# Converting 64-bit weights: ScalarE takes both halves of a chunk at once, and GpSimd takes the integer addition for w_in

## The chip, the cores and the metric

The kernel runs on one core of a Trainium2 chip. The metric is the device time of one execution in microseconds; before the change the median of 3 runs is 906.83 us (906.54 to 906.88). The core's engines run side by side, each with its own queue of instructions in a fixed order: TensorE (PE; its weight loads are PEld), VectorE (DVE), ScalarE (ACT), GpSimd (POOL) and SyncE (SP), which issues most transfers. An instruction at the head of a queue that waits for another engine holds back all that stands behind it. Matmuls write into PSUM; the other tiles live in SBUF, and a tile's slot can be given to a new tile when the last reader of the old one is done.

## The reference

Attention with softmaxes on q (over the head dimension) and on k (over the sequence), then a feed-forward layer with a squared ReLU:

```python
q_s = softmax(q, axis=-1); k_s = softmax(k, axis=2)      # 8 batches, 8 heads, 576 rows, 64 columns
kv  = einsum('bhsd,bhse->bhde', k_s, v)
x   = einsum('bhsd,bhde->bhse', q_s, kv)                 # as 4608 tokens of 512
h   = maximum(x @ w_in, 0.0)                             # w_in  512 x 2048
out = (h * h) @ w_out                                    # w_out 2048 x 512
```

q, k and v are float32. The weights arrive as float64, since their scale factor is a float64, and the kernel reads them as 64-bit words.

## The kernel before

The tokens go in 9 tiles of 512: tile t holds the first 512 rows of batch t, and tile 8 the last 64 rows of all batches. For each tile the FFN runs over 16 chunks `f` of 128 columns of the hidden layer. `first` makes `h` of a chunk (12 matmuls of 128x512: each product is three, with high and low parts of both factors, in the order high x high, high x low, low x high), ScalarE makes `r` (ReLU) from it and VectorE squares it in PSUM; `split_g` makes `gh` on ScalarE and the rest `gl` on VectorE; `second` adds 12 matmuls to four accumulators `acc`, which hold the tile's output. While tile t goes through its FFN, the attention of batch t + 1 is made between the chunks, one pair of heads `p` for each four chunks: `k_max`, `kmT`, `dg` and `kmb` (the maximum of k over the rows, turned and spread by TensorE), `ek` and `kt` (exponentials), `kv`, `qT`, `x`.

The weights are converted once. A chunk has a w_in half and a w_out half, each 128 partitions x 512 words of 64 bits. `load_words` loads them, `scale_words` lets ScalarE scale the high 32 bits as floats (line 130) and the low 32 bits into integers (line 131); `join_words` shifts the high part (line 138, VectorE, into a PSUM bank `up`), puts the sign to it (line 141, VectorE) and adds the low part (line 146 on VectorE for w_in, line 148 on GpSimd for w_out), which gives a float32 `w`; `split_words` casts it to the high part (line 157, ScalarE) and subtracts to get the low part (line 158, GpSimd). A half's first matmuls need the cast, the third and later ones the subtraction. In the trace the loaded words are `raw_i` and `raw_o`, the joined ones `w_i` and `w_o`, the parts `wi` and `wo`. `w` has four buffers of one half each (pool `cvt`), which later serve `store` for the output rows `o`.

`convert` works on one half at a time, a step ahead in scaling and a step behind in splitting. Four calls stand ahead of tile 0, the others in tile 0's loop, two for each chunk. Tile 0's first part (batch 0's attention, 4 chunks' words) is called boot below.

Up to the end of tile 0 a scheduler decides the order in which each engine's queue gets its instructions, from its own estimate of durations; from tile 1 on (`manual_schedule`) the order is that of the code.

```python
for _ in range(2 * LW):
    convert()
```

Of the kernel before, what the change touches and what calls it, by code (L numbers as in the profile page):

```python
# [22 lines left out]
def attention_ffn(  # L23
# [40 lines left out]
    LW = 2  # L64
# [6 lines left out]

    const = ctx.enter_context(tc.tile_pool(name="const", bufs=1))
    att = ctx.enter_context(tc.tile_pool(name="att", bufs=1))
    cvt = ctx.enter_context(tc.tile_pool(name="cvt", bufs=4))
    ffn = ctx.enter_context(tc.tile_pool(name="ffn", bufs=2))
    tiny = ctx.enter_context(tc.tile_pool(name="tiny", bufs=1))
    tiny.tile([P, 32], F32, tag="pad2", name="pad2")
# [29 lines left out]
    wi_h, wi_l, wo_h, wo_l = [], [], [], []  # L107
    raws = []

    def load_words(f):  # L110
        pool = const if f < LATE else late
        for name, src in (
            ("i", w_in[:, f * P:(f + 1) * P].rearrange("(kc p) f -> p kc f", p=P)),
            ("o", w_out[f * P:(f + 1) * P, :]),
        ):
            raw = pool.tile([P, M], U64, tag=f"w{name}{f}", name=f"raw_{name}{f}")
            nc.sync.dma_start(
                out=raw if len(src.shape) == 2 else raw.rearrange("p (a b) -> p a b", b=P),
                in_=src,
            )  # L120
            raws.append((name, f, raw))

    def scale_words(m):
        raw = raws[m][2].bitcast
        hi = raw(F32).rearrange("p (n t) -> p n t", t=2)[:, :, 1]
        lo, lo_i = (raw(t).rearrange("p (n t) -> p n t", t=2)[:, :, 0] for t in (U32, I32))
        nc.scalar.mul(out=hi, in_=hi, mul=2.0**-112)  # L130
        nc.scalar.mul(out=lo_i, in_=lo, mul=2.0**-29)  # L131

    def join_words(m):
        name, f, raw = raws[m]
        lo, hi = (raw.bitcast(I32).rearrange("p (n t) -> p n t", t=2)[:, :, i] for i in range(2))
        w = cvt.tile([P, M], I32, tag="w", name=f"w_{name}{f}")
        ps = bank(f"up_{name}{f}").bitcast(I32)
        nc.vector.tensor_scalar(
            out=ps, in0=hi, scalar1=3, scalar2=None, op0=ALU.logical_shift_left
        )  # L140
        nc.vector.scalar_tensor_tensor(  # L141
            out=ps if name == "i" else w, in0=hi, scalar=-(2**31), in1=ps,
            op0=ALU.bitwise_and, op1=ALU.bitwise_or,
        )
        if name == "i":
            nc.vector.tensor_tensor(out=w, in0=ps, in1=lo, op=ALU.add)
        else:
            nc.gpsimd.tensor_tensor(out=w, in0=w, in1=lo, op=ALU.add)  # L148
        raws[m] = (name, f, w.bitcast(F32))

    def split_words(m):

        name, f, w = raws[m]
        pool = const if f < LATE else late
        parts = pool.tile([P, 2, M], F32R, tag=f"w{name}{f}", name=f"w{name}{f}")
        hi, lo = parts[:, 0, :], parts[:, 1, :]
        nc.scalar.copy(out=hi, in_=w)  # L157
        nc.gpsimd.tensor_tensor(out=lo, in0=w, in1=hi, op=ALU.subtract)
        (wi_h if name == "i" else wo_h).append(hi)
        (wi_l if name == "i" else wo_l).append(lo)  # L160

    converted = [0]

    def convert():

        m = converted[0]
        if m == 0:
            scale_words(0)
        if m + 1 < 2 * NF:
            scale_words(m + 1)  # L170
        if m < 2 * NF:
            join_words(m)
        if 0 < m <= 2 * NF:
            split_words(m - 1)
# [15 lines left out]
    def bank(name):  # L190
        pool, tag = next(banks) if boot_banks else (ps_a, "a")
        return pool.tile([P, M], F32, tag=tag, name=name)
# [416 lines left out]
    for f in range(LW):  # L609
        load_words(f)  # L610
# [29 lines left out]
    for n in range(len(stages) + NP - 1):  # L640
# [3 lines left out]
        if n == len(stages) - 1:  # L644
# [82 lines left out]
    for t in range(B + 1):  # L727
        if t == 1:
            ctx.enter_context(tc.manual_schedule())
        b = t + 1  # L730
        if b <= B:
            x_next = att.tile([P, NP, M], F32, tag="x_next", name=f"x_{b}")
        if b == B:
            nc.sync.dma_start(out=x_next, in_=x_tail)
        acc = [ps_o.tile([P, DM], F32, tag=f"o{c}", name=f"acc_{t}_{c}") for c in range(C)]
        parts = {}
        for f in range(NF):
            h = first(t, f, x)
# [62 lines left out]
```

## Time and profile before

| | |
|---|---|
| median of 3 runs | 906.83 us |
| the profiled execution | 908.01 us |
| its span, first to last instruction | 906.1 us |
| TensorE busy | 868.4 us, 96% of the span, 4028 matmuls |
| VectorE, ScalarE, GpSimd busy | 493.5, 347.6, 176.9 us |
| mean granted TensorE clock | 0.992 |

The profile gives a row for each group of instructions: line, engine, operation, output and inputs by the program's names, shape, count, busy time in us, mean ns of one, and the idle time of the engine just before them with what ended it. In the timeline and the chain of waits a row begins with start and duration in us. The view of stretches gives the busy time of each engine in a piece of the span, with the number of instructions, the granted clock, the share of the transfer engines and GB/s. Busy time of TensorE is that of overlapping matmuls and is not TensorE at its peak.

### The profile page before, as it was taken

The page shows a single profiled execution, that of the slowest core. Times are in us where ns is not written, and L with a number is a line of the kernel's source. Part 1 is how long each engine was busy: PE and PEld are TensorE (multiplying, and loading weights), DVE is VectorE, ACT ScalarE, POOL GpSimd, SP SyncE. Part 2 cuts the span into 40 slices and gives each one's busy share as a digit, 9 for nine tenths or more (in the row PEclk, how much of TensorE's full clock was granted, in tenths as well). Part 3 has the DMA queues.
Part 4 walks back from the last instruction along what each step waited for, and adds up shares of the span by engine and source line. Part 5 has one row for each costly group of instructions (what it writes and reads, how often), then busy time and mean ns, then how long its engine had stood idle before and what let it go on. Part 6 is the DMA issues. An engine that isn't in the chain of part 4 may idle for free.

```text
span 906.1 us, 11603 instructions
## 1 busy us (share of the span) xinstructions
PE 868.4 (96%) x4028; PEld 721.1 (80%) x4028; DVE 493.5 (54%) x964; ACT 347.6 (38%) x667; POOL 176.9 (20%) x214
## 2 busy tenths in 40 slices
PE   3598998999999999999999999999999999999997
PEld 3477777888888888888888888888888888888886
DVE  7978987555564456555564465545555432233222
ACT  3997444333433334333433343333333422232221
POOL 3375664111111111111111101111111100000000
PEclk9799999999999999999999999999999999999999
DMA  8991112211231122111321131112311020000001
GB/s 236 337 398 45 27 37 70 52 38 38 56 84 38 38 46 81 40 33 36 83 48 38 27 100 39 38 37 56 85 38 38 8 93 1 1 34 15 0 1 47
DMA packets 141194, 57.84 MB, mean 64 GB/s; under 512 B 115920, under 2 KB 134352, under 8 KB 141008
## 3 DMA queue, kind: packets, MB, share of 16 engines
q1 hardware_dynamic: 139424, 55.79, 23.0%
q10 hardware_dynamic: 1712, 1.31, 0.5%
q8 instruction: 32, 0.52, 0.2%
q14 instruction: 26, 0.21, 0.1%
HBM read 46.14 MB, written 10.49 MB: 62 GB/s over the span
## 4 chain that ended last, share of the span: by engine, by line
PE 87%; DVE 5%; ACT 4%; DMA 1%; issue 1%; POOL 1%; SPq 0%; DVEq 0%; ACTq 0%
PE h L549 41%; PE acc L571 40%; PE kv L467 3%; PE x L504 2%; PE kv L470 1%; ACT raw_i L130 1%; DMA kt<-in_k_dram 1%; ACT raw_o L130 1%; ACT raw_o L131 1%; ACT raw_i L131 0%; DVE km L363 0%; POOL w_o L148 0%; ACT r L554 0%; ACT gh L563 0%; DVE w_o L141 0%
## 5 line engine op out<-in xcount | busy, mean ns | idle before, releaser
L549 PE MATMUL h<-xh,wi 128*128 128x512 f32 x1152 | 382.2, 395 | 5.6 <-ACT wi L157 3.8
L571 PE MATMUL acc<-wo,gh 128*128 128x512 f32 x1152 | 348.7, 390 | 4.7 <-ACT gh L563 4.7
L549 PEld LDWEIGHTS h<-xh,wi 128*128 128x128 f32 x1152 | 217.4, 189 | 52.2 <-ACT wi L157 5.1
L571 PEld LDWEIGHTS acc<-wo,gh 128*128 128x128 f32 x1152 | 215.0, 188 | 51.7 <-ACT gh L563 7.6
L549 PE MATMUL h<-xl,wi 128*128 128x512 f32 x576 | 225.9, 392 | 0.2 <-DVE xl L540 0.2
L571 PE MATMUL acc<-wo,gl 128*128 128x512 f32 x576 | 216.4, 389 | 0.0
L555 DVE SCALAR_TENSOR_TENSOR h<-h,r 128x512 f32<-128x512 f32 x144 | 99.6, 692 | 125.7 <-ACT r L554 125.6
L564 DVE TENSOR_TENSOR gl<-h,gh 128x512 fp32r<-128x512 f32 x144 | 99.2, 689 | 114.7 <-ACT gh L563 110.4
L554 ACT ACTIVATE r<-h 128x512 f32<-128x512 f32 x144 | 85.6, 594 | 160.4 <-PE h L549 160.3
L563 ACT ACTIVATE gh<-r 128x512 fp32r<-128x512 f32 x144 | 90.8, 631 | 121.6 <-PE acc L571 120.3
L549 PEld LDWEIGHTS h<-xl,wi 128*128 128x128 f32 x576 | 109.0, 189 | 21.7 <-DVE xl L540 0.5
L571 PEld LDWEIGHTS acc<-wo,gl 128*128 128x128 f32 x576 | 108.0, 188 | 22.4
L377 POOL TENSOR_TENSOR k<-k,kmx 128x512 f32<-128x512 f32 x24 | 30.8, 1284 | 171.3 <-issue 135.7
L389 POOL PARTITION_ALL_REDUCE kmx<-km x24 | 17.4, 726 | 194.5 <-DVE km L367 152.8
L328 POOL TENSOR_TENSOR ql<-qT,qh 128x576 fp32r<-128x576 f32 x24 | 34.2, 1425 | 105.2 <-issue 53.0
L300 ACT ACTIVATE q<-q 128x576 f32<-128x576 f32 x24 | 16.5, 686 | 88.5 <-DVE q L297 79.5
L308 DVE SCALAR_TENSOR_TENSOR bsm<-bsm,sw_s 128x18 f32<-128x18 f32 x24 | 4.5, 189 | 62.0 <-DMA sw_s<-bsm 62.0
L467 PEld LDWEIGHTS kv<-v,ek 128*128 128x128 f32 x256 | 34.5, 197 | 2.4 <-ACT ek L418 0.2
L363 DVE TENSOR_REDUCE km<-k 128x128 f32<-128x512 f32 x32 | 33.9, 1059 | 2.1 <-DMA k<-in_k_dram 2.1
L467 PE MATMUL kv<-v,ek 128*128 128x129 f32 x256 | 35.0, 280 | 0.0
L327 ACT CAST qh<-qT 128x576 fp32r<-128x576 f32 x24 | 16.2, 673 | 42.8 <-DVE qT L320 42.8
L296 DVE TENSOR_TENSOR bmx<-bmx,sw_m 128x18 f32<-128x18 f32 x24 | 4.2, 176 | 46.4 <-DMA sw_m<-bmx 46.4
(93 smaller groups left out, 683.7 us busy)
## 6 DMA issues: line engine op xcount, KB each, us to landing
k<-in_k_dram SPq DMA_DIRECT2D x32, 256.0 KB, 2.8
v<-in_v_dram SPq DMA_DIRECT2D x64, 128.0 KB, 2.9
raw_i<-in_moe_w_in_dram SPq DMA_DIRECT2D x16, 512.0 KB, 7.9
raw_o<-in_moe_w_out_dram SPq DMA_DIRECT2D x16, 512.0 KB, 8.9
out_dram<-o SPq DMA_DIRECT2D x32, 256.0 KB, 2.4
q<-in_q_dram SPq DMA_DIRECT2D x96, 72.0 KB, 2.3
sw_m<-bmx SPq DMA_DIRECT2D x96, 2.2 KB, 1.7
sw_s<-bsm SPq DMA_DIRECT2D x96, 2.2 KB, 1.7
```

The costliest lines, as they stand in the source:

```text
L130: nc.scalar.mul(out=hi, in_=hi, mul=2.0**-112)
L328: nc.gpsimd.tensor_tensor(out=ql, in0=qt, in1=qh, op=ALU.subtract)
L363: nc.vector.tensor_reduce(out=km.rearrange("p (h d) -> p h d", h=2), in_=kr.rearrange("p h c d -> p h d c"), op=ALU.max, axis=AX.X,)
L377: eng.tensor_tensor(out=kr, in0=kr, in1=kmx.rearrange("p (h d) -> p h d", h=2).unsqueeze(2).broadcast_to([P, 2, C, D]), op=ALU.subtract,)
L467: nc.tensor.matmul(out=ps[:, 0:W], lhsT=kr[:, c, :], rhs=vr[:, c, :], start=(c == 0), stop=False)
L504: nc.tensor.matmul(out=ps[:, 0:SH], lhsT=a, rhs=c[:, cs], start=(j == 0), stop=(j == 2))
L549: nc.tensor.matmul(out=ps, lhsT=w[f][:, p * P:(p + 1) * P], rhs=m, start=(n == 0), stop=(n == 3 * NP - 1))
L554: nc.scalar.activation(out=r, in_=ps, func=AF.Relu)
L555: nc.vector.scalar_tensor_tensor(out=ps, in0=ps, scalar=0.0, in1=r, op0=ALU.max, op1=ALU.mult)
L563: nc.scalar.activation(out=gh, in_=r, func=AF.Square)
L564: nc.vector.tensor_tensor(out=gl, in0=ps, in1=gh, op=ALU.subtract)
L571: nc.tensor.matmul(out=acc[c], lhsT=a[:, cs], rhs=w[f], start=(f == 0 and n == 0), stop=(f == NF - 1 and n == 2),)
```

## The change

The two halves of a chunk become one tile `raw` (128 x 2 x 512 words) and one tile `w` (two buffers of both halves instead of four of one). `convert` works on a whole chunk. ScalarE's scaling, conversion and cast each take both halves in one instruction of 128x1024. VectorE's shift and sign rows stay one for each half, and both write the sign row's result to `w` in SBUF. The addition runs on GpSimd for both halves, so line 146's addition on VectorE is gone. Two of `store`'s output rows now share a buffer. Two calls of `convert` stand ahead of tile 0 and one in each pass of its loop. In `after` the same lines stand at numbers that differ by a few: the scalings at 130 and 131, shift and sign at 139 and 142, the addition at 146, the cast at 156, the subtraction at 159.

```diff
-    cvt = ctx.enter_context(tc.tile_pool(name="cvt", bufs=4))
+    cvt = ctx.enter_context(tc.tile_pool(name="cvt", bufs=2))
...
-    def scale_words(m):
-        raw = raws[m][2].bitcast
-        hi = raw(F32).rearrange("p (n t) -> p n t", t=2)[:, :, 1]
-        lo, lo_i = (raw(t).rearrange("p (n t) -> p n t", t=2)[:, :, 0] for t in (U32, I32))
+    def scale_words(f):
+        hi = part(f, F32, 1)
         nc.scalar.mul(out=hi, in_=hi, mul=2.0**-112)
-        nc.scalar.mul(out=lo_i, in_=lo, mul=2.0**-29)
+        nc.scalar.mul(out=part(f, I32, 0), in_=part(f, U32, 0), mul=2.0**-29)
...
-        w = cvt.tile([P, M], I32, tag="w", name=f"w_{name}{f}")
...
-        nc.vector.scalar_tensor_tensor(
-            out=ps if name == "i" else w, in0=hi, scalar=-(2**31), in1=ps,
-            op0=ALU.bitwise_and, op1=ALU.bitwise_or,
-        )
-        if name == "i":
-            nc.vector.tensor_tensor(out=w, in0=ps, in1=lo, op=ALU.add)
-        else:
-            nc.gpsimd.tensor_tensor(out=w, in0=w, in1=lo, op=ALU.add)
+        w = cvt.tile([P, 2, M], I32, tag="w", name=f"w_{f}")
+        for h in range(2):
...
+            nc.vector.scalar_tensor_tensor(
+                out=w[:, h, :], in0=hi[:, at], scalar=-(2**31), in1=ps,
+                op0=ALU.bitwise_and, op1=ALU.bitwise_or,
+            )
+            nc.gpsimd.tensor_tensor(
+                out=w[:, h, :], in0=w[:, h, :], in1=lo[:, at], op=ALU.add
+            )
...
-        nc.scalar.copy(out=hi, in_=w)
-        nc.gpsimd.tensor_tensor(out=lo, in0=w, in1=hi, op=ALU.subtract)
+        parts = pool.tile([P, 2, 2, M], F32R, tag=f"w{f}", name=f"w{f}")
+        nc.scalar.copy(out=parts[:, :, 0, :], in_=w)
+        for h, (his, los) in enumerate(((wi_h, wi_l), (wo_h, wo_l))):
+            hi, lo = parts[:, h, 0, :], parts[:, h, 1, :]
+            nc.gpsimd.tensor_tensor(out=lo, in0=w[:, h, :], in1=hi, op=ALU.subtract)
...
-        o = cvt.tile([P, DM], F32, tag="w", name=f"o_{t}_{c}")
+        if c % 2 == 0:
+            made["o"] = cvt.tile([P, 2, DM], F32, tag="w", name=f"o_{t}_{c}")
+        o = made["o"][:, c % 2, :]
...
-    for _ in range(2 * LW):
+    for _ in range(LW):
         convert()
...
-            if t == 0 and f + LW < NF:
-                convert()
```

How the queues change is shown at two places. First GpSimd's queue where the conversion begins, at the end of boot. Before (the digit behind `w_o`, `wi`, `wo` is the chunk; `qn` belongs to batch 1's attention):

```order
L277 TENSOR_TENSOR qn_1_0_576<-q_1_0_372,sm_1_0_577 128x2x4x64
L148 TENSOR_TENSOR w_o0_483<-w_o0_483,raw_o0_146 128x512
L158 TENSOR_TENSOR wi0_488<-w_i0_476,wi0_488 128x512
L148 TENSOR_TENSOR w_o1_503<-w_o1_503,raw_o1_150 128x512
L158 TENSOR_TENSOR wi1_508<-w_i1_493,wi1_508 128x512
L158 TENSOR_TENSOR wo0_498<-w_o0_483,wo0_498 128x512
L158 TENSOR_TENSOR wo1_566<-w_o1_503,wo1_566 128x512
```

And now, where `w_0` is the joined chunk 0 and `w0` its parts, and x2 stands for both halves:

```order
L146 TENSOR_TENSOR w_0_470<-w_0_470,raw_0_144 128x512 x2
L278 TENSOR_TENSOR qn_1_0_563<-q_1_0_370,sm_1_0_564 128x2x4x64
L146 TENSOR_TENSOR w_1_481<-w_1_481,raw_1_147 128x512
L159 TENSOR_TENSOR w0_490<-w_0_470,w0_490 128x512 x2
L146 TENSOR_TENSOR w_1_481<-w_1_481,raw_1_147 128x512
L146 TENSOR_TENSOR w_2_543<-w_2_543,raw_2_376 128x512 x2
L159 TENSOR_TENSOR w1_552<-w_1_481,w1_552 128x512 x2
```

Chunk 0's subtraction for w_in stood behind one addition; now it stands behind three and `qn`, and chunk 1's behind six additions and chunk 0's subtractions.

Second, ScalarE's queue in the middle of tile 0, around chunk 6 (`r_0_6` and `gh_0_6` are tile 0's, the rows of `q_1`, `ek_1` and `kt_1` batch 1's; the engine behind "waits" is the one that releases the row). Before:

```order
L157 CAST wo6_923<-w_o6_888 128x512 [waits Pool_49]
L418 ACTIVATE ek_1_1_883<-k_1_1_638 128x2x4x64 [waits DVE_49]
L422 ACTIVATE kt_1_364<-kt_1_364 64x128 [waits DVE_49]
L554 ACTIVATE r_0_6_969<-h_0_6_956 128x512 [waits PE_49]
L563 ACTIVATE gh_0_6_998<-r_0_6_969 128x512 [waits Activation_49]
L157 CAST wi7_953<-w_i7_918 128x512 [waits DVE_49]
L157 CAST wo7_983<-w_o7_948 128x512 [waits Pool_49]
L157 CAST wi8_1040<-w_i8_978 128x512 [waits DVE_49]
```

And now:

```order
L156 CAST w6_879<-w_6_800 128x2x512 [waits Pool_49]
L430 ACTIVATE q_1_2_901<-q_1_2_901 128x512 [waits DMAHW1_49,Pool_49]
L419 ACTIVATE ek_1_1_846<-k_1_1_619 128x2x4x64 [waits DVE_49]
L423 ACTIVATE kt_1_362<-kt_1_362 64x128 [waits DVE_49]
L555 ACTIVATE r_0_6_916<-h_0_6_903 128x512 [waits PE_49]
L564 ACTIVATE gh_0_6_949<-r_0_6_916 128x512 [waits Activation_49]
L156 CAST w7_933<-w_7_870 128x2x512 [waits Pool_49]
```

The casts of w_in waited for VectorE's addition and now wait, with those of w_out, for GpSimd's second one; the casts of chunks 7 and 8 still stand behind `gh` of chunk 6.

More of the change, by code (lines that the diff above doesn't have):

```diff
@@ L111, in load_words @@
         pool = const if f < LATE else late
[L112 to L119, printed above, removed]
-            )
-            raws.append((name, f, raw))
@@ L126, in scale_words @@
-    def scale_words(m):
-        raw = raws[m][2].bitcast
-        hi = raw(F32).rearrange("p (n t) -> p n t", t=2)[:, :, 1]
-        lo, lo_i = (raw(t).rearrange("p (n t) -> p n t", t=2)[:, :, 0] for t in (U32, I32))
[L130 to L135, printed above, removed]
-        w = cvt.tile([P, M], I32, tag="w", name=f"w_{name}{f}")
-        ps = bank(f"up_{name}{f}").bitcast(I32)
-        nc.vector.tensor_scalar(
-            out=ps, in0=hi, scalar1=3, scalar2=None, op0=ALU.logical_shift_left
-        )
-        nc.vector.scalar_tensor_tensor(
-            out=ps if name == "i" else w, in0=hi, scalar=-(2**31), in1=ps,
-            op0=ALU.bitwise_and, op1=ALU.bitwise_or,
-        )
-        if name == "i":
-            nc.vector.tensor_tensor(out=w, in0=ps, in1=lo, op=ALU.add)
-        else:
-            nc.gpsimd.tensor_tensor(out=w, in0=w, in1=lo, op=ALU.add)
-        raws[m] = (name, f, w.bitcast(F32))
@@ L151, in split_words @@
-    def split_words(m):
-        name, f, w = raws[m]
-        pool = const if f < LATE else late
[L155 to L160, printed above, removed]
+        raw = pool.tile([P, 2, M], U64, tag=f"w{f}", name=f"raw_{f}")
@@ new lines, in load_words, with part @@
+        nc.sync.dma_start(
+            out=raw[:, 0, :].rearrange("p (a b) -> p a b", b=P),
+            in_=w_in[:, f * P:(f + 1) * P].rearrange("(kc p) f -> p kc f", p=P),
+        )
+        nc.sync.dma_start(out=raw[:, 1, :], in_=w_out[f * P:(f + 1) * P, :])
+        raws.append(raw)
+    def part(f, dtype, i):
+        raw = raws[f].rearrange("p h n -> p (h n)").bitcast(dtype)
+        return raw.rearrange("p (n t) -> p n t", t=2)[:, :, i]
+    def scale_words(f):
+        hi = part(f, F32, 1)
+        nc.scalar.mul(out=hi, in_=hi, mul=2.0**-112)
+        nc.scalar.mul(out=part(f, I32, 0), in_=part(f, U32, 0), mul=2.0**-29)
@@ new lines, in join_words @@
+    def join_words(f):
+        lo, hi = part(f, I32, 0), part(f, I32, 1)
+        w = cvt.tile([P, 2, M], I32, tag="w", name=f"w_{f}")
+        for h in range(2):
+            at = slice(h * M, (h + 1) * M)
+            ps = bank(f"up_{f}_{h}").bitcast(I32)
+            nc.vector.tensor_scalar(
+                out=ps, in0=hi[:, at], scalar1=3, scalar2=None, op0=ALU.logical_shift_left
+            )
+            nc.vector.scalar_tensor_tensor(
[4 more added lines that the diff above has]
+                out=w[:, h, :], in0=w[:, h, :], in1=lo[:, at], op=ALU.add
+            )
+        raws[f] = w.bitcast(F32)
@@ L162, in attention_ffn, with split_words @@
+    def split_words(f):
+        w = raws[f]
+        pool = const if f < LATE else late
+        parts = pool.tile([P, 2, 2, M], F32R, tag=f"w{f}", name=f"w{f}")
[3 more added lines that the diff above has]
+            nc.gpsimd.tensor_tensor(out=lo, in0=w[:, h, :], in1=hi, op=ALU.subtract)
+            his.append(hi)
+            los.append(lo)
     converted = [0]
@@ L164, in convert @@
     def convert():
-        m = converted[0]
-        if m == 0:
+        f = converted[0]
+        if f == 0:
             scale_words(0)
[L169 to L174, printed above, removed]
+        if f + 1 < NF:
+            scale_words(f + 1)
+        if f < NF:
+            join_words(f)
+        if 0 < f <= NF:
+            split_words(f - 1)
         converted[0] += 1
```

## The prediction

> **What bounds the kernel now.** I read the stretches first: the busy time of each engine in five pieces of the span, cut where the first matmul of tile 0's FFN starts (41.98), where its first chunk enters the second product (51.87), where the seventh `h` is done (87.48), and where tile 1 runs freely (158.27).
>
> ```profile
> core 0: us, PE busy (x) PEld busy (x) DVE busy (x) ACT busy (x) POOL busy (x), PEclk, DMA share, GB/s
> 0.00:41.98 41.98, 17.98 (x94) 14.60 (x94) 36.68 (x107) 26.25 (x58) 13.48 (x30) 0.92 0.92 277
> 41.98:51.87 9.89, 9.46 (x28) 6.75 (x28) 9.41 (x16) 9.65 (x19) 9.89 (x9) 0.66 1.06 402
> 51.87:87.48 35.61, 34.05 (x157) 27.34 (x157) 26.28 (x52) 32.12 (x63) 19.85 (x21) 1.00 0.56 201
> 87.48:158.27 70.79, 64.44 (x306) 52.21 (x306) 60.73 (x110) 32.70 (x62) 40.33 (x39) 1.00 0.18 46
> 158.27:906.10 747.83, 742.46 (x3446) 620.17 (x3445) 360.44 (x682) 246.83 (x468) 93.34 (x118) 1.00 0.18 43
> ```
>
> After 158.27 TensorE is busy 742.46 of 747.83 us and no line of the change runs there except `store`, so that part stays. The weights' conversion lies in the first four pieces, and the result is decided there. Busy time flatters TensorE, because its instructions overlap; what the work costs is read from the chain of waits where nothing interrupts it:
>
> ```profile
> 164.28 2.72 PE acc L571 x12
> 167.00 0.89 PE kv L467 x8
> 168.11 2.77 PE h L549 x12
> 173.60 0.79 PE x L504 x6
> ```
>
> One chunk of weights is 12 `h` and 12 `acc` matmuls, 2 x 2.72 = 5.44 us; one pair of heads adds 1.03 (`kv`, up to 168.03), 0.79 (`x`) and, by my estimate from the neighbouring rows, 0.6 for transposes and the `kmb`. A chunk with its share of attention is about 6.0 us.
>
> From 51.87 to 87.48 TensorE does 5 `h`, 6 `acc`, one `kv`, one `x` and small rows: 11 x 2.72 + 2.5 = 32.4 us of 35.6, so 3.2 us are lost. From 87.48 to 158.27 it does 9 `h` and 11 matmuls of tile 1, 10 `acc`, three pairs of heads: 24.5 + 2.5 + 27.2 + 7.4 = 61.6 us of 70.8, so 9.2 us are lost. The waits from 32 to 158 us, in total and times, say to whom:
>
> ```profile
> PE acc L571 <- ACT gh L563: 4.7, 6, 1.4
> PE h L549 <- ACT wi L157: 3.8, 2, 3.3
> ...
> PE kmb L408 <- DVE dg L400: 1.4, 1, 1.4
> ```
>
> TensorE waits mostly for `gh`, and `gh` is late for two different reasons. In the third piece ScalarE has hardly a gap (32.12 of 35.61). In the fourth it has time, but stands still in its queue:
>
> ```profile
> 86.23 0.62 ACT L157 CAST wo<-w_o 128x512 fp32r<-128x512 f32 x1 [2.24 <-POOL w_o L148]
> ...
> 87.69 0.60 ACT L554 ACTIVATE r<-h 128x512 f32<-128x512 f32 x1
> ```
>
> The cast of `wo` waits 2.24 us for GpSimd's addition; `ek`, `kt`, `r` and `gh` stand behind it. And GpSimd itself waits for VectorE, which is the fullest helper there (60.73 of 70.79):
>
> ```profile
> core 0: us, POOL busy (x), PEclk, DMA share, GB/s
> 41.50:149.50 108.00, 69.75 (x66) 0.97 0.36 123
> ...
> L148 POOL TENSOR_TENSOR w_o<-w_o,raw_o 128x512 int32<-128x512 int32 x16 | 21.2, 1324 | 20.4 <-DVE w_o L141 20.4
> L158 POOL TENSOR_TENSOR wo<-w_o,wo 128x512 fp32r<-128x512 f32 x16 | 20.8, 1301 | 8.7 <-ACT wo L157 8.7
> L158 POOL TENSOR_TENSOR wi<-w_i,wi 128x512 fp32r<-128x512 f32 x16 | 20.7, 1297 | 4.9 <-ACT wi L157 4.8
> ```
>
> **The change: ScalarE.** 32 scalings, 32 conversions and 32 casts of 128x512 become 16 of each at 128x1024, a width that no row shows.
>
> ```profile
> 49.55 0.67 ACT L130 ACTIVATE raw_i<-raw_i 128x512 f32<-128x512 f32 x1
> 50.11 0.67 ACT L131 ACTIVATE raw_i<-raw_i 128x512 int32<-128x512 uint32 x1
> 50.67 0.61 ACT L157 CAST wi<-w_i 128x512 fp32r<-128x512 f32 x1
> ...
> L327 ACT CAST qh<-qT 128x576 fp32r<-128x576 f32 x24 | 16.2, 673 | 42.8 <-DVE qT L320 42.8
> L492 ACT CAST kvh<-kv 128x128 fp32r<-128x128 f32 x32 | 9.5, 298 | 39.8 <-DVE kv L482 39.8
> ```
>
> The slope is (673 - 298) / 448 = 0.84 ns per element. L130 and L131 follow one another every 0.56 us, so at double width every 0.56 + 0.43 = 0.99, and a merged pair saves 0.13; a merged cast saves about 0.09. The bounds are one whole start saved, 0.56 - 0.43 = 0.13, and nothing saved; a loss has no reason, for 128x576 lies on the line from 128x128. I take 0.13, the value of the nearest row. In the third piece ScalarE runs 17 pairs of L130 and L131 and 8 casts:
>
> ```profile
> L130 ACT ACTIVATE raw_o<-raw_o 128x512 f32<-128x512 f32 x9 | 6.2, 692 | 0.0
> ...
> L130 ACT ACTIVATE raw_i<-raw_i 128x512 f32<-128x512 f32 x8 | 5.6, 696 | 0.0
> ...
> L157 ACT CAST wo<-w_o 128x512 fp32r<-128x512 f32 x5 | 3.2, 633 | 2.2 <-POOL w_o L148 2.2
> ...
> L157 ACT CAST wi<-w_i 128x512 fp32r<-128x512 f32 x3 | 1.9, 631 | 0.2 <-DVE w_i L146 0.2
> ```
>
> That is 17 merges (of 17 L130 and as many L131) x 0.13 + 4 x 0.09 = 2.6 us less on the engine that sets `gh`, within the 3.2 that TensorE loses: **-2.6**. The Trainium skill's page "ScalarE: Activation LUTs", section "What ACT_TABLE_LOAD costs", gives 186 ns + 0.833 ns per element with an overlap of 93 ns, by which a merge saves 93 ns; the trace's slope agrees, and the term would be 21 x 0.093 = 2.0.
>
> **The start.** In the new order VectorE builds both halves of chunk 0 before it touches chunk 1.
>
> ```profile
> 36.90 0.66 DVE L138 TENSOR_SCALAR up_i<-raw_i 128x512 int32<-128x512 int32 x1
> ...
> 37.74 0.68 DVE L138 TENSOR_SCALAR up_o<-raw_o 128x512 int32<-128x512 int32 x1
> ...
> 40.23 0.67 DVE L146 CUSTOM_DVE_ANT_0 w_i<-raw_i,up_i 128x1024 uint16<-128x1024 uint16 x1
> 40.83 0.67 DVE L141 SCALAR_TENSOR_TENSOR w_o<-raw_o,up_o 128x512 int32<-128x512 int32 x1
> ```
>
> Before, VectorE ended chunk 0's `w_in` at 40.83. Behind it now go the two shifts shown, one more 0.6 us row of chunk 1, three smaller attention rows (about 1.3) and the addition itself (0.6); ahead of it comes `w_o`'s second row (0.6): about 37.2. GpSimd's rows follow one another every 1.26 us:
>
> ```profile
> 41.58 1.31 POOL L148 TENSOR_TENSOR w_o<-w_o,raw_o 128x512 int32<-128x512 int32 x1 [2.73 <-DVE w_o L141]
> 42.84 1.28 POOL L158 TENSOR_TENSOR wi<-w_i,wi 128x512 fp32r<-128x512 f32 x1
> ```
>
> So its addition ends at 38.5, the double cast (0.52 + 0.43) at 39.5, and the first `h` starts about 2.5 us earlier. But GpSimd then has `qn` (1.0), the addition for chunk 1 and only then the subtraction whose result the third matmul needs: 42.1. The other half's subtraction, three more additions and chunk 1's subtraction follow: 42.1 + 5 x 1.26 = 48.4 is when `h_1` can go on, whatever the clock (0.66 here) makes of `h_0`. Its last 10 matmuls take 2.3; `acc` starts at about 50.9 instead of 51.87: **-1.0**.
>
> **VectorE and GpSimd.** VectorE loses 16 additions, GpSimd gains 16.
>
> ```profile
> L146 DVE CUSTOM_DVE_ANT_0 w_i<-raw_i,up_i 128x1024 uint16<-128x1024 uint16 x16 | 10.8, 677 | 0.8
> L400 DVE TENSOR_SCALAR dg<-ident,kc 128x128 f32<-128x128 f32 x4 | 3.0, 754 | 0.0
> ```
>
> VectorE: -16 x 0.6 = -9.6, some 6 of it in the fourth piece (about 10 additions); its queue is what made GpSimd wait 20.4 us. GpSimd: + 16 x 1.26 = 20.2, so 69.75 + 20.2 + 1.0 (`qn`, now behind the first addition) = 91 us. Its load per chunk is 4 x 1.26 and 0.6 of attention = 5.6, just under TensorE's 6.0. Starting at 37.2 it ends at 128.2 if it never waits. TensorE, if it never waited after 50.9, would be done with its two pieces at 50.9 + 32.4 + 61.6 = 144.9; behind chunk 15's subtraction it has 10 `h`, 24 `acc`, one `x` and the 11 of tile 1, 11.0 us, so it needs that at 133.9. So 5.7 us of GpSimd idling are free, against 38 us now.
>
> I followed the queues row by row in the new order with these durations. GpSimd nearly always finds the next chunk's addition to do while a subtraction waits for its cast. The double cast waits for two additions, and what stands behind it at chunk 6 is `q`, `ek`, `kt` and `r`; but later casts stand behind `gh`, and VectorE's row that waits for GpSimd to free `w` (with `h` and `gl` behind it) comes early enough. TensorE's loss in the fourth piece falls from 9.2 to about 2. Such a walk has no slack for hand-overs and for rows that collide with GpSimd (`dg` takes 754 ns on average in this stretch), so I give back 2: **-5.2**.
>
> The Trainium skill's "SBUF — State Buffer", section "SBUF: two separate sides", says that VectorE and GpSimd take a shared port pair in turns, for a whole instruction. `dg`'s 754 ns fits that; by this rule a busier GpSimd lengthens such rows, at most one 1.3 us instruction for each of four `dg` on TensorE's path, 5 us if all were bare, which the 2 above stand for.
>
> **`store`.** Two `o` rows share a buffer, but a slot is used again a tile later, 87 us (16 x 5.44) on: nothing. Without that cover it is one landing a tile:
>
> ```profile
> out_dram<-o SPq DMA_DIRECT2D x32, 256.0 KB, 2.4
> ```
>
> **The sum.** -2.6 - 1.0 - 5.2 = -8.8 us on the profiled span of 906.1 (that execution took 908.01, the median run 906.83): 906.83 - 8.8 = **898.0**.
>
> **Rivals.** *GpSimd becomes the bound* (slower). Its rows cost 1324 against 677 ns; it is in series with ScalarE (add, add, cast, subtract, subtract) in one fixed queue, and VectorE now waits for it to free `w` (two buffers). If it kept its 38.3 us of idling, tile 0 would end at 128.2 + 38.3 + 11.0 = 177.5 instead of 158.27: 926. It decides from 158.27 - 11.0 - 128.2 = 19 us of idling, where the gain is gone. For it: 20.4 of the waits come from VectorE, whose rows are not shorter, only fewer. Against: those waits are VectorE's queue, which gets 9.6 us. The rule in the skill's "GPSIMD Engine Reference", section 4.1, to keep elementwise work off GpSimd because it is about twice as slow for two inputs, says the same; the ratio here is 1.96. 0.13.
> *ScalarE alone gains*: the fourth piece stays as it is, because the casts wait for both additions: -1.0 - 2.6, 903.2. 0.15.
> *The halves cancel*: GpSimd's lag eats the rest, 905 to 908.6. 0.07.
> *Double width saves nothing* on ScalarE: 900.6, inside the forecast's range.
>
> **How the numbers follow.** Forecast 0.65, from 891 (no loss left in either piece and a start at 39.5, -14.9, and one more for the clock there) to 902.5. The range 891 to 907 takes in the ScalarE-only case and the cancelling one; left out are the slower case and little below. Within 0.2% (1.8 us, about what can be told from no change) 0.08, faster 0.79, slower 0.13.
>
> **What would show it.** The 128x1024 rows near 1.1 us; the first `h` near 39.5 with a wait for GpSimd right behind it; `h_6` done near 84; GpSimd over 85% busy from 40 to 130 with its last subtraction before 138; tile 1 free near 149; `gh` no longer TensorE's first waiter. Wrong it is if GpSimd still idles over 19 us there or TensorE waits for its subtractions chunk after chunk.

## The result, and the profile after

| | before | after |
|---|---|---|
| median of 6 runs each on the same chip, us | 907.00 (906.54 to 907.76) | 901.14 (900.48 to 902.20) |
| ratio, with its 95% interval | | 0.9936 (0.9924 to 0.9949) |
| the profiled execution, us | 908.01 | 902.16 |
| its span, us | 906.1 | 900.4 |

The change makes the kernel 0.64% faster. The forecast was 898.0, the range 891 to 907: the direction and about two thirds of the size are right (5.9 us of 8.8), and the measured time lies 3.1 us above the forecast.

The stretches of the changed kernel, cut at the same events as in the prediction: first `h` at 40.26, first chunk in the second product at 51.36, `h_6` done at 85.16, tile 1 running at 151.05. The columns are the pieces' bounds and length, then busy time and number of instructions of each engine.

```profile
core 0: us, PE busy (x) PEld busy (x) DVE busy (x) ACT busy (x) POOL busy (x), PEclk, DMA share, GB/s
0.00:40.26 40.26, 17.55 (x94) 14.01 (x95) 35.41 (x103) 23.33 (x44) 16.18 (x32) 0.91 0.92 279
40.26:51.36 11.10, 8.92 (x28) 6.29 (x28) 9.55 (x16) 11.10 (x16) 11.10 (x10) 0.70 1.06 397
51.36:85.16 33.80, 33.44 (x160) 27.45 (x158) 26.20 (x50) 30.14 (x42) 26.81 (x26) 1.00 0.59 212
85.16:151.05 65.89, 63.01 (x307) 52.33 (x307) 53.56 (x100) 30.74 (x52) 49.07 (x46) 1.00 0.17 40
151.05:900.40 749.35, 743.08 (x3446) 620.07 (x3444) 361.21 (x682) 245.98 (x468) 93.17 (x118) 1.00 0.18 43
```

The third piece went from 35.61 to 33.80, the fourth from 70.79 to 65.89, the two before them from 51.87 to 51.36: 7.2 us in all. But the last piece, which "stays", went from 747.83 to 749.35. TensorE's waits from 32 to 158 us (total, times, longest) are now these; the first two lie ahead of 40 us, in boot:

```profile
PE x L505 <- ACT kvh L493: 3.9, 2, 2.8
PE x L505 <- DVE kvl L494: 2.3, 2, 1.7
PE h L550 <- POOL w L159: 2.2, 2, 1.1
PE kv L468 <- ACT gh L564: 1.5, 1, 1.5
PE kmb L409 <- DVE dg L401: 1.2, 1, 1.2
...
PE acc L572 <- ACT gh L564: 0.4, 1, 0.4
```

`acc` waited 4.7 us for `gh` before; 0.4 is left. The groups of GpSimd, ScalarE and VectorE from 32 to 155 us (busy us, mean ns, then the idle time before them and what ended it):

```profile
L146 POOL TENSOR_TENSOR w<-w,raw 128x512 int32<-128x512 int32 x32 | 41.6, 1313 | 10.6 <-DVE w L142 10.4
L159 POOL TENSOR_TENSOR w<-w,w 128x512 fp32r<-128x512 f32 x32 | 40.9, 1302 | 2.4 <-ACT w L156 2.2
...
L156 ACT CAST w<-w 128x1024 fp32r<-128x1024 f32 x16 | 16.9, 1054 | 8.6 <-POOL w L146 8.5
L130 ACT ACTIVATE raw<-raw 128x1024 f32<-128x1024 f32 x14 | 16.3, 1164 | 0.1
L131 ACT ACTIVATE raw<-raw 128x1024 int32<-128x1024 uint32 x14 | 16.1, 1150 | 0.0
...
L401 DVE TENSOR_SCALAR dg<-ident,kc 128x128 f32<-128x128 f32 x4 | 4.0, 1009 | 0.1
```

GpSimd's two operations now run 32 times each and wait 13.0 us, where its three groups waited 34.0 before. The start, in TensorE's timeline (start, duration, operation, wait and releaser):

```profile
40.26 0.80 PE L550 MATMUL h<-xh,w 128*128 128x512 f32 x1 [0.49 <-ACT w L156]
42.51 1.22 PE L550 MATMUL h<-xh,w 128*128 128x512 f32 x2 [1.03 <-POOL w L159]
48.81 0.74 PE L550 MATMUL h<-xh,w 128*128 128x512 f32 x2 [1.15 <-POOL w L159]
```

The first `h` comes 1.7 us earlier, its third matmul waits for GpSimd, and so does `h_1`, as foreseen.

### The profile page after: what moved, and what is told of

Same layout as the page of the kernel before. It is cut to its first block, busy times and chain, and to the rows that moved or that the text cites. A ratio compares the mean times of both kernels' runs of the same rounds, so it can differ in the third digit from the quotient of the medians.

```text
span 900.4 us, 11575 instructions
## 1 busy us (share of the span) xinstructions
PE 866.0 (96%) x4028; PEld 720.2 (80%) x4028; DVE 485.9 (54%) x948; ACT 341.3 (38%) x619; POOL 196.3 (22%) x230
## 4 chain that ended last, share of the span: by engine, by line
PE 88%; DVE 4%; DMA 4%; SPq 1%; issue 1%; POOL 1%; ACT 1%; DVEq 0%; ACTq 0%; POOLq 0%
PE acc L572 41%; PE h L550 41%; PE kv L468 3%; PE x L505 2%; DMA raw<-in_moe_w_out_dram 1%; DMA sw_m<-bmx 1%; PE kv L471 1%; SPq L286 1%; DVE up L139 1%; DMA k<-in_k_dram 1%; POOL w L146 1%; DMA kt<-in_k_dram 1%; SPq L225 0%; DVE gl L565 0%; DMA raw<-in_moe_w_in_dram 0%
## 5 line engine op out<-in xcount | busy, mean ns | idle before, releaser
L550 PE MATMUL h<-xh,w 128*128 128x512 f32 x1152 | 381.8, 395 | 3.4 <-POOL w L159 2.2
L572 PE MATMUL acc<-w,gh 128*128 128x512 f32 x1152 | 348.3, 390 | 0.4 <-ACT gh L564 0.4
L550 PEld LDWEIGHTS h<-xh,w 128*128 128x128 f32 x1152 | 217.0, 189 | 50.9 <-POOL w L159 3.3
L572 PEld LDWEIGHTS acc<-w,gh 128*128 128x128 f32 x1152 | 215.4, 188 | 44.9 <-ACT gh L564 0.7
L550 PE MATMUL h<-xl,w 128*128 128x512 f32 x576 | 225.7, 392 | 0.0
L572 PE MATMUL acc<-w,gl 128*128 128x512 f32 x576 | 216.8, 389 | 0.0
L572 PEld LDWEIGHTS acc<-w,gl 128*128 128x128 f32 x576 | 108.1, 188 | 22.5
L550 PEld LDWEIGHTS h<-xl,w 128*128 128x128 f32 x576 | 108.9, 189 | 21.0
L146 POOL TENSOR_TENSOR w<-w,raw 128x512 int32<-128x512 int32 x32 | 41.6, 1313 | 10.6 <-DVE w L142 10.4
L159 POOL TENSOR_TENSOR w<-w,w 128x512 fp32r<-128x512 f32 x32 | 40.9, 1302 | 2.4 <-ACT w L156 2.2
```

What stands on the lines that cost most here:

```text
L146: nc.gpsimd.tensor_tensor(out=w[:, h, :], in0=w[:, h, :], in1=lo[:, at], op=ALU.add)
L159: nc.gpsimd.tensor_tensor(out=lo, in0=w[:, h, :], in1=hi, op=ALU.subtract)
L550: nc.tensor.matmul(out=ps, lhsT=w[f][:, p * P:(p + 1) * P], rhs=m, start=(n == 0), stop=(n == 3 * NP - 1))
L572: nc.tensor.matmul(out=acc[c], lhsT=a[:, cs], rhs=w[f], start=(f == 0 and n == 0), stop=(f == NF - 1 and n == 2),)
```

## The experiments

Twelve kernels ran, each timed beside the kernel before on the same chip. The table has medians, the ratio to the kernel before with its interval, and from the profiled execution three distances to the kernel before in us: where ScalarE's row on tile 0's `h_0` starts (before: 49.05), the same on tile 1's `h_8` (200.95) and on the last `h` (892.96). Negative is earlier. The last column is the mean granted TensorE clock, from the lowest to the highest of a kernel's executions; the kernel before has 0.990 to 0.994 in its own. A thousandth of it is about 0.9 us of TensorE's full speed.

| kernel | median us | ratio (95%) | h_0 | tile 1, h_8 | last h | clock |
|---|---|---|---|---|---|---|
| the changed kernel, first profile | 901.14 | 0.9936 (0.9924 to 0.9949) | -1.0 | -7.4 | -5.7 | 0.991 to 0.992 |
| e1_after_again | 900.80 | 0.9931 (0.9919 to 0.9944) | -0.5 | -6.9 | -5.5 | 0.991 to 0.992 |
| e2_wide_only | 909.01 | 1.0015 (1.0006 to 1.0024) | +0.4 | +1.1 | +2.0 | 0.991 to 0.992 |
| e3_add_only | 901.67 | 0.9940 (0.9928 to 0.9953) | +2.2 | -4.9 | -5.5 | 0.990 to 0.992 |
| e4_cast_halves | 904.06 | 0.9962 (0.9950 to 0.9975) | -1.3 | -4.1 | -4.0 | 0.991 to 0.992 |
| e5_scale_halves | 907.08 | 0.9999 (0.9990 to 1.0008) | +0.5 | -1.0 | -1.3 | 0.989 to 0.991 |
| e6_wout_on_dve | 902.19 | 0.9944 (0.9932 to 0.9957) | -0.8 | -5.9 | -6.0 | 0.991 to 0.993 |
| e7_mix4 | 903.80 | 0.9964 (0.9950 to 0.9978) | -0.5 | -3.7 | -4.3 | 0.990 to 0.992 |
| e8_pe_fill16 | 901.38 | 0.9936 (0.9924 to 0.9949) | -1.4 | -6.4 | -6.7 | 0.990 to 0.992 |
| e9_after_order_before | 912.80 | 1.0066 (1.0054 to 1.0079) | +3.0 | +5.0 | +4.9 | 0.986 to 0.989 |
| e10_before_order_after | 905.78 | 0.9985 (0.9976 to 0.9994) | +0.5 | -1.2 | -1.6 | 0.989 to 0.992 |
| e11_wide_order_after | 907.59 | 1.0004 (0.9994 to 1.0013) | +0.2 | +0.1 | +0.9 | 0.988 to 0.990 |
| e12_wide_sbuf | 905.12 | 0.9979 (0.9971 to 0.9988) | -1.3 | -3.7 | -4.1 | 0.988 to 0.992 |

### What is lost behind tile 0: e1 and e8

`e1` is the changed kernel as it is.

> The changed kernel once more, unaltered. In the profiled execution of it each hidden unit block from tile 1 on stood 7.4 us earlier than in the kernel before, until two late landings of the small transfers sw_m and sw_s (at 575 to 580 and at 633 to 638 us) cost 0.70 and 1.0 us. Theory: these landings are scatter from execution to execution, so another profile shows tile 0 shorter by the same 7.2 to 7.4 us, but not these two losses at these two places, and a span nearer to 899. Rival: the earlier end of tile 0 causes them, so they come back at the same places with 0.7 and 1.0 us and the span is again 900.4 or near.

The rival held: at the same two places the second profile lost 1.0 and 1.1 us. What happens at the first of them is seen on VectorE, where line 297 waits for the landing of `sw_m` (timeline of the changed kernel):

```profile
579.79 0.18 DVE L297 TENSOR_TENSOR bmx<-bmx,sw_m 128x18 f32<-128x18 f32 x1 [4.06 <-DMA sw_m<-bmx]
```

The view of the tile `sw_m` from 574.4 to 581 us has the time from issue to landing of its four transfers:

```profile
DMA to landing us min/median/max: 1.7/1.7/3.4
```

And the transfer queues from 577 to 580 us (packets, MB, share):

```profile
q8 instruction: 1, 0.02, 1.8%
```

The middle landing takes 1.7 us, the longest 3.4, and a transfer of instructions (16 KB, queue q8, 32 times in the span) runs just then, at 577.65. `gl` stands behind line 297 in VectorE's queue, and the next `h` waits for it. The kernel before passes the place with 2.44 us of waiting instead of 4.06 (its line 296, at 585.53); there the 16 KB come between 585.55 and 585.80, when the wait is over. `e8` moves these transfers and nothing else.

```diff
     def first(t, f, x):
...
+        if t == 1 and f == 1:
+            for _ in range(16):
+                nc.tensor.matmul(
+                    out=ps[0:32, 0:32], lhsT=ident[:, 0:32], rhs=ident[:, 0:32],
+                    start=True, stop=True,
+                )
```

> The changed kernel with 16 small matmuls more (32 rows by 32, written over at once) ahead of one h in tile 1, nothing else moved: TensorE's instruction stream is shifted by 32 instructions, so each later 16 KB instruction transfer comes about 3.6 us earlier in the work. They cost some 1 to 3 us themselves. Theory (in the changed kernel these transfers fall between the issue and the landing of a small transfer at 577.6 and 635.9 us, which then lands after 3.3 to 3.4 us instead of 1.7, and TensorE loses 0.7 and 1.0 us): both landings take 1.7 us again and both losses are gone, so that the distance to the kernel before, once the cost of the 16 matmuls is in, does not change by 0.7 to 1.1 us at unit 88 to 90 and at 97 to 100. Rival (the late landings have another cause): both come back with 0.7 to 1.1 us each.

The instruction transfers moved further than expected, to 571.5 and 625.1 us, ahead of the small transfers. VectorE's row at the same place in `e8`'s timeline:

```profile
578.63 0.18 DVE L297 TENSOR_TENSOR bmx<-bmx,sw_m 128x18 f32<-128x18 f32 x1 [2.43 <-DMA sw_m<-bmx]
```

And the landing times of `sw_m` there, from 574.8 to 580 us:

```profile
DMA to landing us min/median/max: 1.7/1.7/1.7
```

The second place, too, is back to 1.8 us at most. The distance to the kernel before stays at -6.9 us past the first place (-7.4 to -6.7 in the changed kernel) and goes to -6.7 past the second (-6.7 to -5.7 there). The 16 matmuls cost 1.3 us at tile 1 (-7.7 at its first `h`, -6.4 at `h_8`), so the median gains nothing; the cause is shown for these two places all the same.

### The parts alone: e2 and e3

`e2` keeps w_in's addition on VectorE, in the wide kernel:

```diff
+            nc.vector.scalar_tensor_tensor(
+                out=ps if h == 0 else w[:, h, :], in0=hi[:, at], scalar=-(2**31), in1=ps,
...
+            if h == 0:
+                nc.vector.tensor_tensor(out=w[:, h, :], in0=ps, in1=lo[:, at], op=ALU.add)
```

> ScalarE's three operations take both halves of a chunk, but the addition for w_in stays on VectorE (and its input in PSUM). Theory (two separate gains): the gain of the third stretch (tile 0 from the first h to h_6, 1.8 us) and at most the 0.5 us of the start are here, the 4.9 us of the fourth stretch are not: about 904.7, between 903.5 and 906. Rival A (the moved addition alone carries the gain): 907, within 0.5 of the kernel before. Rival B (wide ScalarE work alone carries it): 901, as the changed kernel.

`e3` is the kernel before with w_in's addition moved:

```diff
-            out=ps if name == "i" else w, in0=hi, scalar=-(2**31), in1=ps,
+            out=w, in0=hi, scalar=-(2**31), in1=ps,
...
-        if name == "i":
-            nc.vector.tensor_tensor(out=w, in0=ps, in1=lo, op=ALU.add)
-        else:
-            nc.gpsimd.tensor_tensor(out=w, in0=w, in1=lo, op=ALU.add)
+        nc.gpsimd.tensor_tensor(out=w, in0=w, in1=lo, op=ALU.add)
```

> The kernel before, but with the addition for w_in on GpSimd as well; ScalarE's operations keep to one half each. Theory (two separate gains): the fourth stretch's 4.9 us are here, the 1.8 us of the third are not: about 902 to 903. Rival A (the move alone): 901 or below. Rival B (wide ScalarE work alone): 907, or slower by GpSimd's two extra microseconds in the start, to 909.

Not two gains that add up: `e2` lies above all three of its values, and `e3` just under its theory's. The move alone brings 5.9 us (907.54 to 901.67), the wide operations alone lose 1.5. On top of the move, taking whole chunks helps in the start alone: `e3` starts tile 0 3.2 us later than the changed kernel, and at tile 1 it is 2.5 us behind, so within tile 0 it is not slower. It ends level because the changed kernel loses 1.7 us behind tile 0, as shown above, and `e3` nothing there.

### Single operations back: e4, e5, e6, e7

`e4` and `e5` split the cast and the scalings again:

```diff
-        nc.scalar.copy(out=parts[:, :, 0, :], in_=w)
+        for h in range(2):
+            nc.scalar.copy(out=parts[:, h, 0, :], in_=w[:, h, :])
```

> The changed kernel with the cast alone split again into two halves, so that the cast of w_in's half waits for one GpSimd addition and not for two, and its subtraction can start 2 us earlier in the start. Theory: ScalarE pays 16 times 0.09 us, of which 7 lie in the third stretch (0.6 us), and the start gains back up to 0.6 us: 900.5 to 902, no difference that can be told from the changed kernel. Rival (the wait of the wide cast for both additions is what holds tile 0 in the fourth stretch): 899 or below.

```diff
+        lo, lo_i = part(f, U32, 0), part(f, I32, 0)
+        for at in (slice(0, M), slice(M, 2 * M)):
+            nc.scalar.mul(out=hi[:, at], in_=hi[:, at], mul=2.0**-112)
+            nc.scalar.mul(out=lo_i[:, at], in_=lo[:, at], mul=2.0**-29)
```

> The changed kernel with the two scalings split again into halves (four operations of 128x512 a chunk), the cast left wide and both additions on GpSimd. Theory (the moved addition carries nearly all, the wide scalings save ScalarE 0.08 us each, 14 of them before h_6): 901 to 902.5. Rival (the wide scalings are worth as much as the wide cast, whose splitting cost 3 us): 903.5 to 905.

In `e6` and `e7` the condition for VectorE's addition in `e2` reads `h == 1`, and `h == 0 and f % 4 == 3`.

> The changed kernel with the two additions exchanged: w_in's on GpSimd, w_out's back on VectorE (16 of each, as before the change). Theory (VectorE's load is what the moved addition relieves, whichever matrix it is for): no gain, 907 to 910, as with w_in's addition kept on VectorE. Rival (it is the path of w_in that matters, because h waits for w_in and GpSimd and ScalarE get it sooner or with less queueing): 901 to 903.

> The changed kernel with w_in's addition kept on VectorE in every fourth chunk (f = 3, 7, 11, 15): 28 additions on GpSimd, 4 on VectorE. Theory (each addition taken off VectorE is worth the same, 8 us over 16): 902.5 to 903.5. Rival (GpSimd is near its limit, so that the first few back on VectorE are free or a gain): 901 or below.

`e4` lost 3.3 us, `e5` 6.3 against `e1`: both expectations missed, and by more than the ScalarE time that the splits add (16 times 0.1 and 32 times 0.085 us, 1.6 and 2.7; worked out below). The 6.3 us of `e5` cannot be the price of narrow scalings, since `e3`, in which everything is narrow, takes 901.7. `e7` lies just above its theory: 4 of the 16 additions back on VectorE cost 3.0 us, not 2. `e6` misses the theory as clearly, and its rival, that the path of w_in matters, held: VectorE has 16 additions again and 5.1 us of the gain are there. Its stretch of tile 0 (columns as above):

```profile
48.20:152.90 104.70, 100.59 (x476) 81.94 (x477) 91.02 (x168) 64.83 (x99) 62.51 (x61) 1.00 0.32 103
```

VectorE is busy for 91.02 of 104.70 us, 87%; in the kernel before it is 89.63 of 109.80 (49.00 to 158.80), 82%. A less loaded VectorE is therefore not what the gain needs. What all these kernels share is that the scheduler, which goes by its own estimate of durations, gave each another order in tile 0, TensorE's queue included. So the order had to be held.

### The order held: e9, e10, e11, e12

The attention's and the FFN's TensorE instructions are the same in all these kernels, so an order can be carried over. Each instruction of tile 0 is made to stand behind its predecessor of the wanted order, without a wait:

```diff
+        mine = [i for i in traced if str(i.engine).split(".")[-1] == engine and not _quiet(i)]
+        order = [k for k in order if k < len(mine)]
+        for a, b in zip(order, order[1:]):
+            tc.add_manual_dep(
+                mine[b], mine[a].name,
+                mybir.DependencyInfo(mybir.DependencyClass.NoSync, mybir.DependencyReason.DATA),
+                reason="keep_order",
+            )
```

> The changed kernel, but TensorE's instructions of tile 0 stand in the order that they have in the kernel before (each is made to stand behind its predecessor of that order; no wait is added). Theory (the gain is in the work: what the engines beside TensorE do and how long): 901 to 903. Rival (the gain is in the order that the scheduler found for TensorE, whatever the work): 905.5 to 908.

> The kernel before, but TensorE's instructions of tile 0 stand in the order that they have in the changed kernel. Theory (work): 906 to 909, no gain. Rival (order): 901 to 903. Between the two, both have a part, and the distance to the kernel before is the order's.

With TensorE's order of the kernel before, the changed work is slower than before, by 5.6 us: neither theory had that. TensorE's waits in `e9` from 40 to 165 us:

```profile
PE h L550 <- ACT w L156: 7.1, 6, 2.2
PE kmT L397 <- DVE w L142: 3.0, 1, 3.0
PE acc L572 <- ACT gh L564: 2.0, 2, 1.5
```

That order asks for the next `h` earlier than the wide cast, which needs both halves, can serve it. Part of the loss is TensorE's granted clock, which is lower in the profile of `e9` than in that of the kernel before: 0.50 against 0.92 from 48 to 52 us, 0.73 from 112 to 116 and 0.84 from 116 to 120 against 1.00. By my estimate (4 us times each difference) that is up to 3.4 of the 5.6 us. The other way round, the new order alone gives the old work 1.5 us, between the two theories; here too the clock is lower at one place (0.86 from 88 to 100 us, up to 1.7 us by the same estimate).

The last two kernels take the changed kernel's order of TensorE and of ScalarE, and their edit differs from it only in w_in's addition. VectorE's and GpSimd's queues are still the scheduler's, and some of VectorE's rows do stand elsewhere. `e11` has the addition as `e2`; `e12` lets the sign row write to SBUF:

```diff
-                out=ps if h == 0 else w[:, h, :], in0=hi[:, at], scalar=-(2**31), in1=ps,
+                out=w[:, h, :], in0=hi[:, at], scalar=-(2**31), in1=ps,
...
-                nc.vector.tensor_tensor(out=w[:, h, :], in0=ps, in1=lo[:, at], op=ALU.add)
+                nc.vector.tensor_tensor(out=w[:, h, :], in0=w[:, h, :], in1=lo[:, at], op=ALU.add)
```

> ScalarE's three operations wide, w_in's addition on VectorE as in e2_wide_only (909.0), but TensorE's and ScalarE's instructions of tile 0 stand in the changed kernel's order. The one difference from the changed kernel that is left is on which engine w_in's addition runs. Theory (work: VectorE's addition ahead of w_out's two operations holds back GpSimd and with it the wide cast): 906 to 909. Rival (e2 lost by its order, not by the addition): 901 to 903.

With these two orders held, w_in's addition on VectorE costs 6.8 us (907.59 against 900.80), as the theory had it. Most of it is lost at one place, around chunk 6: ScalarE's row on `h_6` comes 1.2 us later than in the changed kernel (-1.1 against -2.3, measured as in the table), the one on `h_7` 6.4 us later (+4.8 against -1.6). `e2` loses as much in small waits, none over 1.5 us from 40 to 165 us, so `e11` does not tell how much of `e2`'s loss was its order. TensorE's timeline in `e11`:

```profile
90.51 1.85 PE L471 MATMUL kv<-v,ek 128*128 128x129 f32 x7 [3.97 <-ACT w L159]
```

VectorE's there:

```profile
85.16 1.27 DVE L139 TENSOR_SCALAR up<-raw 128x512 int32<-128x512 int32 x2
...
87.01 0.68 DVE L142 SCALAR_TENSOR_TENSOR up<-raw,up 128x512 int32<-128x512 int32 x1
...
89.74 0.67 DVE L147 CUSTOM_DVE_ANT_0 w<-raw,up 128x1024 uint16<-128x1024 uint16 x1
```

In the changed kernel, TensorE:

```profile
86.79 1.13 PE L468 MATMUL kv<-v,ek 128*128 128x129 f32 x8 [1.47 <-ACT gh L564]
```

And VectorE:

```profile
84.02 1.28 DVE L139 TENSOR_SCALAR up<-raw 128x512 int32<-128x512 int32 x2
...
85.32 1.23 DVE L142 SCALAR_TENSOR_TENSOR w<-raw,up 128x512 int32<-128x512 int32 x2
```

`up`, `kmT`, `kmb`, `qT`, `kv` and `x` share two PSUM banks (pool `ps_a`). Two shift rows take both. In the changed kernel the two sign rows read them out at once: they end at 86.55, and `kv` starts at 86.79. In `e11` one bank is read last by VectorE's addition, which ends at 90.41 (89.74 + 0.67), and `kv` starts at 90.51; the row names the cast as releaser, but the cast ended at 89.52.

The wait is followed by a lower granted clock. The stretch from 88 to 100 us in `e11`, four microseconds of it, and the same 12 us in the changed kernel (columns as above, the clock is the third number from the end):

```profile
88.00:100.00 12.00, 9.49 (x36) 8.09 (x37) 9.95 (x18) 3.07 (x5) 6.73 (x8) 0.72 0.15 31
92.00:96.00 4.00, 4.00 (x13) 3.32 (x13) 3.65 (x10) 0.30 (x1) 1.43 (x3) 0.50 0.33 74
```

```profile
88.00:100.00 12.00, 11.80 (x57) 9.47 (x56) 11.51 (x23) 4.92 (x9) 12.00 (x14) 1.00 0.21 51
```

At 0.72 of the clock, 12 us are worth up to 3.4 us less, by my estimate. So of the 5.2 us lost between `h_6` and `h_7`, 2.5 are the longer wait and most of the rest is the clock. All executions of `e11` have a lower mean clock than those of the changed kernel (see the table).

> As e11_wide_order_after (907.6: w_in's addition on VectorE, orders of TensorE and ScalarE held to the changed kernel's), but the or writes w in SBUF and the addition reads and writes w there, so that the PSUM bank of the shifted words is free after the or and not only after the addition. VectorE has the same 16 additions. In the changed kernel the bank is free after the or too. Theory (the addition on VectorE costs by holding one of the two PSUM banks that kmT, kmb, qT, kv and x of tile 0 also use): 901 to 903.5. Rival (it costs by VectorE's time and by letting GpSimd and the cast start later): 906.5 to 909, as e11.

`e12` frees the bank after the sign row: `kv` starts at 86.57 there, the clock stays at 1.00 from 88 to 100 us, and the median is 2.5 us lower than `e11`'s, intervals apart. These 2.5 us are what the edit is worth with all that follows from it, the clock and the time lost behind tile 0 included (1.2 us in `e11`'s profile, none in `e12`'s); the bank's share alone was not measured. In the place of `kv`, `qT` waits in `e12`:

```profile
92.37 0.66 PE L448 MATMUL qT<-ident,qn 128*128 128x128 f32 x4 [2.16 <-DVE w L142]
```

Its bank, too, is read by a sign row, which stands in VectorE's queue behind an addition of 1.68 us. For the addition is dearer in `e12`; its group in `e11`, and then in `e12`:

```profile
L147 DVE CUSTOM_DVE_ANT_0 w<-raw,up 128x1024 uint16<-128x1024 uint16 x16 | 10.9, 678 | 0.4
```

```profile
L147 DVE CUSTOM_DVE_ANT_0 w<-raw,w 128x1024 uint16<-128x1024 uint16 x16 | 17.1, 1068 | 0.1
```

The mean of 1068 ns mixes two cases. Seven of the 16 rows take 0.67 to 0.69 us, as in `e11`; the other nine take 0.81 to 1.74 us, and each of them ends 0.5 to 0.6 us behind the end of a subtraction that GpSimd was already running. One such row with GpSimd's row beside it, from `e12`:

```profile
128.67 1.60 DVE L147 CUSTOM_DVE_ANT_0 w<-raw,w 128x1024 uint16<-128x1024 uint16 x1
...
128.44 1.29 POOL L162 TENSOR_TENSOR w<-w,w 128x512 fp32r<-128x512 f32 x1
```

And from `e11`, where one input lies in PSUM:

```profile
132.50 0.67 DVE L147 CUSTOM_DVE_ANT_0 w<-raw,up 128x1024 uint16<-128x1024 uint16 x1
...
132.27 1.30 POOL L162 TENSOR_TENSOR w<-w,w 128x512 fp32r<-128x512 f32 x1
```

So both answers have a part. The edit frees the bank and in exchange puts nine additions behind GpSimd; 4.3 us remain to the changed kernel (905.12 against 900.80). About 2.1 of them are lost between `h_6` and `h_7`, where `qT` waits; how the others divide was not tried. `e6` also has the addition reading a bank, for w_out, and loses little: at the same place one row stands between the sign row (85.23) and the addition (86.42) in VectorE's queue, against three in `e11` (87.01 and 89.74). What the bank costs thus seems to hang on VectorE's order, which no run held.

## Why the prediction was right, and where it was not

- **The start, -1.0**: measured -0.5 (`acc` at 51.36 instead of 51.87). Each step came as told, 0.4 to 0.8 us later: first `h` 40.26 (39.5), third matmul 42.51 (42.1), `h_1` 48.81 (48.4). `e3` shows that it hangs on taking whole chunks: half by half, the move makes the start later.
- **ScalarE, -2.6**: the third piece shrank by 1.8. The size of the saving was off: the wide scalings follow one another every 1.03 and 1.04 us (49.99, 51.02, 52.06), not 0.99, so a merge saves 0.085 and not 0.13; two narrow casts take 1.03 us in `e4` (48.25 to 49.28) and a wide one 0.94 (48.52 to 49.46), so a merged cast saves 0.1, about as told; 17 x 0.085 + 4 x 0.1 = 1.85. The rule of 93 ns from the Trainium skill's "ScalarE: Activation LUTs", which gave 2.0, was nearer. That 1.85 meets the 1.8 is luck as far as the runs show. From `h_0` to `h_6` the changed kernel gains 1.3 us on the kernel before (-1.0 to -2.3), `e3` with narrow operations 1.0 (+2.2 to +1.2), and `e2` with wide ones loses 1.6 (+0.4 to +2.0). The step that took the narrow operations to be what holds the third piece is therefore not borne out; each of these kernels has its own order, so it is not refuted either.
- **VectorE and GpSimd, -5.2**: the fourth piece shrank by 4.9. The size is right and the waits went where the prediction sent them. That the move is what brings it is borne out: `e3`, the move alone, gains 6.0 us from `h_6` to tile 1 (+1.2 to -4.8). The reason was incomplete. "VectorE: -16 x 0.6 = -9.6" was to be the cause; `e6` gains 5.1 us without that relief. `e11` and `e12` show two costs of w_in's addition on VectorE that no engine's busy time contains: the shared PSUM bank that it held, and the lower clock behind the wait. The prediction had a term for neither.
- **The order.** The prediction walked through the new order and put the gain to the engines. `e9` and `e10` show that neither half stands alone: old work in TensorE's new order 905.8, new work in its old order 912.8, both new 900.8. Without the lower clock (up to 1.7 us in `e10`, up to 3.4 in `e9`) the first would gain at most half and the second still nothing. The gain belongs to the pair, and the sum of separate terms came out as near as it did partly by luck.
- **"That part stays"**: this step failed, by 1.7 us in the profiled execution (-7.4 at tile 1's `h_8`, -5.7 at the last `h`). Shifted instruction transfers delay two small ones; `e8` removes both delays.
- **GpSimd as the bound**: it did not come to it. From 41.50 to 139.50 GpSimd is busy 85.02 of 98.00 us, so 13.0 us of idling stand against the 19 from which it decides; its last subtraction ends at 139.3 (138 was named). The rule of the Trainium skill's "GPSIMD Engine Reference", section 4.1, holds in its ratio (1313 ns against 677) and not in its consequence here. `dg` takes 1009 ns instead of 754, in the direction that the skill's "SBUF — State Buffer", section "SBUF: two separate sides", has: 4 x 0.26 = 1.0 us, inside the 2 given back. Three of the four rows end 0.1 us behind the end of a GpSimd row that ran when they started (101.35 + 1.16 against 102.43, for one).

From 898.0 to 901.1 the pieces miss by 0.8 in the third, 0.5 in the start, 0.3 in the fourth, and 1.5 behind tile 0. Open is why `e4`, `e5` and `e7` lose as much as they do: each has its own order, and none was repeated with the order held. Open is also what sets the clock back in tile 0: `qT` waits 2.0 us in `e10` and 2.2 us in `e12`, and only in `e10` is the clock lower behind it.

## What to carry to other kernels

Where a scheduler sets the order, two versions differ in their work and in their order, and one edit can give each sign: carry one order over to both before a difference of some us is put to an operation. When an operation is moved to another engine, look not only at busy time but at what the old one held while it waited, here one of two PSUM banks. A wait of TensorE can cost more than its length: look at the granted clock of the stretch behind it. And a queue that waits for small transfers can lose a few us far behind the edit, because the edit shifts when instructions are fetched.

## What the hardware showed that was not expected

A 16 KB instruction transfer between the last issue and the landing of a 2.2 KB transfer makes that landing 3.3 to 3.7 us instead of 1.7 to 1.8. Of 14 landings looked at in seven profiles (the two places in the kernel before, the changed one, `e1`, `e2`, `e3`, `e4` and `e8`), the six late ones have such a transfer in between, and the eight others have it in the last 0.4 us, behind the landing, or not near. Elsewhere in the same traces the delay is smaller in part: around 606 us in the changed kernel three landings take 2.1 to 3.0 us with such a transfer in between. The Trainium skill's "Runtime: NRT & Kernel Launch", section "Instruction fetch mechanics", says that instructions come in 16 KiB blocks of 256 and that crossing a block is mostly hidden. The trace agrees on the blocks (32 of 16 KB on q8, as many as 4028 matmuls with their weight loads make); the cost here was not TensorE's own but that of other transfers, 1.7 us.

VectorE's exact integer addition (128x1024 uint16) takes 0.67 to 0.69 us wherever its inputs lie, but with both in SBUF (`e12`) it waits for a GpSimd subtraction that is already running, and ends 0.5 to 0.6 us behind it; so in nine of ten cases, and in the tenth (40.28 us) the subtraction took 2.1 us instead of 1.3. With one input in PSUM (`e11`) the two run side by side.

TensorE's granted clock fell to 0.50 a second time within tile 0 in `e11` (92 to 96 us, behind a wait of 3.97 us), and it was 0.73 from 112 to 116 us in `e9` and 0.75 from 96 to 100 us in `e10`, behind waits of 2.2 and 2.0 us. In the profiles of the kernel before and of the changed one, where no wait of TensorE from 52 us to the end of tile 0 is over 1.5 us, it stays at 1.00 there.
